# Two attention blocks on one core: eleven loads of V described as 8 blocks of 4 rows instead of 32 rows

## The chip, the core and the metric

The kernel runs on one core of one Trainium2 chip. Beside the four compute engines (PE, the matrix engine; DVE, the vector engine; ACT, the scalar engine; POOL) the core has a sequencer SP, which here issues nearly all transfers, and sixteen DMA engines that carry them between the chip's memory (HBM) and the on-chip buffers (SBUF). The metric is the device time in microseconds; the time before is the median of three runs, 840.8 us (840.2 to 841.24).

## The reference

Two attention blocks, A and B, on separate inputs; their outputs stand side by side in the result. Both project a batch of 16 x 32 tokens to 32 query heads, attend to a cache of 1024 keys with heads of 128, and project back to 1024 columns. They differ in the cache: A has 4 key/value heads, each used by 8 query heads; B has 32 of its own.

```python
q = (x @ wq).reshape(B, Sq, H, Dh).transpose(0, 2, 1, 3)
scores = jnp.einsum("bhqd,bhkd->bhqk", q, k_cache) * (Dh ** -0.5)
p = softmax(scores)
o = jnp.einsum("bhqk,bhkd->bhqd", p, v_cache)
out = o.transpose(0, 2, 1, 3).reshape(B, Sq, H * Dh) @ wo
...
return jnp.concatenate([a, b], axis=-1)
```

All data are bf16. B's two caches are 134 MB each (16 x 32 x 1024 x 128 x 2 bytes), A's 17 MB each, so the kernel reads 338 MB in one pass.

## The kernel before

The work is cut into 128 steps for each attention. A step of B, a *quad*, handles four (batch, head) pairs with 32 queries each, which together fill the 128 partitions: scores into two PSUM banks (L1040), the row maximum on DVE (L1051), the exponential on ACT (L1064), a transposition of the probabilities on PE (L1076), their copy to SBUF (L655), the product with V (`st_pvB`, L1109), the normalisation and a transposition of the result. After each group of quads the output projection follows (L827). A's steps are alike and are set between B's.

The order of the instructions on each engine is not the order of the source. `list_schedule` simulates the engines with a table of durations and picks, engine by engine, what goes next; SP's queue is ordered by it too. It knows a transfer by its name and its bytes (`dma_time`, by `vb_dma` for the loads here), not by how its source is described. Semaphores are then placed by `finalize`.

**The loads.** SP issues about a thousand transfers, all on one queue (`qSPDynamicHW`), each as soon as its buffer is free; it waits in order, so a load whose buffer is not free holds up all those behind it. `load` (L625) is the helper for the caches and the output weights. It regards `fold` neighbouring rows of the source as one longer row. For a tile of V, 128 rows of 2048 bytes (the 8 keys of a partition, 128 values each), with `fold` 4, the source is described as 32 rows of 8192 bytes, and the destination as 128 partitions of 2048 bytes. The source is one piece of 256 KB without gaps in any case.

**V of B.** There are 512 such loads, numbered `y` from 0 to 511; quad `t` uses y = 4t to 4t + 3, one for each of its four pairs. `st_dmaVB` (L965) emits them. `home_v` gives the buffer: up to y = 419 one of twelve slots of `VB_sb`, later also the room that the token buffers leave free (`xT_sb`, `QT_sb`), and for the last eight loads that of K tiles (`KB_sb`). The four loads of a quad share a semaphore (`sem_v`), and PE waits for all four before L1109. A slot is loaded again when PE has finished the product that read it.

Of the kernel before, what the change touches and what calls it, by code (L numbers as in the profile page):

```python
# [7 lines left out]
ALU = alu_op_type.AluOpType  # L8
# [549 lines left out]
def build(nc, pa, pb, out):  # L558
# [9 lines left out]
    NCH = Sk // P  # L568
# [4 lines left out]
    MS = 4  # L573
# [17 lines left out]
    pr = Prog()  # L591
    stack = contextlib.ExitStack()
    with stack:
# [28 lines left out]

        psum = ps("psum", [P, 8, 512], F32)

        def load(e, dst, src, fold):  # L625

            if fold == 1:
                return e.dma_start(dst, src)
            return e.add_instruction(mybir.InstDMACopy(  # L629
                name=nc.get_next_instruction_name(), engine=mybir.EngineType.SP, queue="qSPDynamicHW", mode="Copy",  # L630
                ins=e.lower_ap_dma(src.rearrange("(p r) x -> p (r x)", r=fold)), outs=e.lower_ap_dma(dst), cce_op=ALU.bypass))

        def bank(v):
            return psum[:, v.idx, :]
# [158 lines left out]
        def wo_loadA(s_):  # L793
            wo = pa["wo"]
            for h_ in range(HS):
                r0 = (s_ * HS + h_) * Dh

                def th(h_=h_, r0=r0):
                    pr.add("sp", lambda e: load(e, woA_sb[:, h_, :], wo[r0:r0 + Dh, :], 4),
                           writes=[("woA", h_)], dma_key=f"woA{h_}", name="woA_dma", dur=Dh * D * 2, wtag={("woA", h_): s_})  # L800
                lazy_push(("wo", 0, s_), th)

        def wo_loadB(m_):
            wo = pb["wo"]
            for h_ in range(MS):
                r0 = (m_ * MS + h_) * Dh

                def th(h_=h_, r0=r0):
                    pr.add("sp", lambda e: load(e, woB_sb[:, h_, :], wo[r0:r0 + Dh, :], 4),
                           writes=[("woB", h_)], dma_key=f"woB{h_}", name="woB_dma", dur=Dh * D * 2, wtag={("woB", h_): m_})  # L810
                lazy_push(("wo", 1, m_), th)
# [79 lines left out]
        def st_dmaKA(q):  # L891
            if not q.kv_new:
                return
            sl = q.kvslot
            pr.add("sp", lambda e: load(e, KA_sb[:, sl, :, :].rearrange("p c d -> p (c d)"), pa["k"][q.b, q.s].rearrange("(p c) d -> p (c d)", c=NCH), 4),
                   writes=[("KA", sl)], dma_key=f"ka{sl}", name="ka_dma", dur=Sk * Dh * 2, wtag={("KA", sl): q.kid})
# [26 lines left out]
        def home_v(y):  # L923
            x, h = y // 2, y % 2
            if x >= V_LAST:
                return (("KB", "KBh")[h], kb_of(x - 8))
            if x < XV:
                return ("VB", 2 * (x % NVB) + h)
            r = (x - XV) % (NVB + 4)
            return ("xV" if r < 2 else "QV", 2 * (r % 2) + h) if r < 4 else ("VB", 2 * ((XV + r - 4) % NVB) + h)  # L930
# [19 lines left out]
        def tile_v(y):  # L950
            kind, sl = home_v(y)
            if kind == "xV":
                return xT_sb[:, 1, :, :].rearrange("p (i j) t -> p i (j t)", i=4)[:, sl, :]
            if kind == "QV":
                return QT_sb[:, 0, :, :, :].rearrange("p (i b) a q -> p i (b a q)", i=4)[:, sl, :]
            if kind in ("KB", "KBh"):
                h = int(kind == "KBh")
                return KB_sb[:, sl, h * NCH * Dh:(h + 1) * NCH * Dh]
            return VB_sb[:, sl, :]

        def sem_v(y):
            kind, sl = home_v(y - y % 4)
            return {"VB": sl // 4, "xV": NVB, "QV": NVB + 1}.get(kind, NVB + 2 + sl)

        def st_dmaVB(y):  # L965
            kind, sl = home_v(y)
            q, x = quadsB[y // 4], y % 4
            pr.step, was = 2 * ((y // 2 - NVB) // 4) if y // 2 >= NVB else pr.step, pr.step
            pr.add("sp", lambda e: load(e, tile_v(y), pb["v"][q.b0 + x // 2, q.m * MS + 2 * (x % 2) + q.e].rearrange("(p s) d -> p (s d)", s=NCH), 4),
                   writes=[(kind, sl)],  # L970
                   dma_key="v%d" % sem_v(y), name="vb_dma", dur=Sk * Dh * 2, wtag={(kind, sl): ("V", y)})
            pr.step = was
# [182 lines left out]
        def pairB(n):  # L1155
            qs = [quadsB[2 * n], quadsB[2 * n + 1]]
            for x in range(4):
                st_ktrB(4 * n + x)
            if n == 0:
                for x in range(4, NKB):  # L1160
                    st_dmaKB(x)
            st_scoresB(qs)
            while k_next[0] < min(2 * NIT, 4 * n + 4 + NKB + (4 if n >= LATE else 0)):
                st_dmaKB(k_next[0])
                k_next[0] += 1
            if 4 * n == V_LAST - 8:
                for y in range(8):
                    st_dmaVB(2 * V_LAST + y)
            for q in qs:
                st_max(q)  # L1170
                st_exp(q)
                st_ptr(q)
                st_pev(q)
                st_pvB(q)
                while v_next[0] < min(2 * V_LAST, 4 * q.t + 4 + 2 * NVB + (8 if n >= LATE else 0)):
                    st_dmaVB(v_next[0])
                    v_next[0] += 1
                st_recip(q)
                st_norm(q)
                st_otr(q)  # L1180
# [34 lines left out]
        for y in range(8):  # L1215
            st_dmaVB(y)
# [86 lines left out]
        if SCHED:  # L1303
            pr = pr.list_schedule()
# [41 lines left out]
```

## Time and profile before

| | |
|---|---|
| median of three runs | 840.8 us (840.2 to 841.24) |
| the profiled execution, its own time | 841.83 us |
| its span, first to last instruction | 840.0 us |
| granted clock of PE, mean | 0.99 |
| read from HBM | 337.64 MB |
| loads of V of B into `VB_sb` | 468 of 256 KB, median 7.5 us from issue to landing |

The profile is one execution on the chip. Its page gives the busy time of each engine, the span in forty slices, the DMA queues with the share of sixteen engines' time that their packets took, the chain of waits that ended last, and the costliest groups of instructions; finer views answer for a stretch of time, a tile or a line of the source. Queue q1 is SP's; q0 carries the seven stores that POOL issues; q8 and q14 bring the engines' own instructions. A packet of 4 bytes is the completion that one DMA engine writes to a load's semaphore when its share is done, and in this trace there are sixteen for each of the 1009 transfers that SP and POOL issue (16144 packets under 512 bytes). "DMA share" in a window is the mean busy share of the sixteen DMA engines; a packet is counted where it starts, so in short windows the share can pass 1.

### The profile page before, as it was taken

How to read it: one execution, taken by the hardware profiler on the slowest of the kernel's cores; microseconds unless marked ns; L12 is line 12 of the kernel's file. 1: busy time of each engine (PE TensorE's matmuls, PEld its weight loads, DVE VectorE, ACT ScalarE, POOL GpSimd, SP SyncE). 2: the span in 40 equal slices, each digit the busy share in tenths (PEclk: the TensorE clock that was granted, in tenths of full speed). 3: DMA queues.
4: the chain of work that ended last, by engine and by line, in shares of the span. 5: the costliest groups of instructions: out<-in, count | busy, mean ns of one | idle time of the engine just before them, and what ended most of it. 6: DMA issues, size and time to landing. Idle time of an engine off the chain costs nothing.

```text
span 840.0 us, 29458 instructions
## 1 busy us (share of the span) xinstructions
PE 732.0 (87%) x12732; PEld 470.6 (56%) x12864; DVE 721.5 (86%) x1021; ACT 608.4 (72%) x1356; POOL 5.0 (1%) x15
## 2 busy tenths in 40 slices
PE   6979989898889889988998988988889988789776
PEld 3446655655656555655556555565646656466553
DVE  1688888979979888988998898998899889988994
ACT  4368878867768785877678786685867877687764
POOL 0000000000000000000000000000000000000000
PEclk9999999999999999999999999999999999999999
DMA  9999999999999999999999999999999999999995
GB/s 336 420 419 414 416 418 418 414 414 410 404 418 415 416 417 419 396 415 416 418 410 410 411 415 419 417 415 402 405 419 400 415 417 419 416 418 417 418 390 224
DMA packets 65104, 341.68 MB, mean 407 GB/s; under 512 B 16144, under 2 KB 16400, under 8 KB 26064
## 3 DMA queue, kind: packets, MB, share of 16 engines
q1 hardware_dynamic: 64416, 337.97, 98.6%
q8 instruction: 101, 1.65, 0.8%
q0 software_dynamic: 560, 1.84, 0.5%
q14 instruction: 27, 0.22, 0.1%
HBM read 337.64 MB, written 2.10 MB: 404 GB/s over the span
## 4 chain that ended last, share of the span: by engine, by line
PE 37%; DMA 22%; DVE 21%; ACT 12%; SPq 4%; issue 3%; ACTq 0%
DMA KB_sb<-in_B_k_cache_dram 14%; DVE stat L1051 9%; DVE KB_sb L991 9%; ACT P_sb L1064 8%; PE psum L1076 7%; PE psum L827 6%; DMA VB_sb<-in_B_v_cache_dram 5%; PE psum L1040 5%; PE psum L758 4%; PE psum L1109 3%; PE psum L1096 3%; SPq L629 3%; PE psum L739 2%; PE psum L1010 2%; ACT PT_sb L655 2%
## 5 line engine op out<-in xcount | busy, mean ns | idle before, releaser
L1051 DVE TENSOR_REDUCE stat<-psum 128x1 f32<-128x1024 f32 x256 | 301.8, 1206 | 38.5 <-PE psum L1040 22.7
L1064 ACT ACTIVATE P_sb<-psum,stat 128x1024 bf16<-128x1024 f32 x246 | 275.0, 1120 | 56.8 <-DVE stat L1051 55.3
L991 DVE STREAM_TRANSPOSE KB_sb<-KB_sb 128x1024 f32<-128x1024 f32 x240 | 287.2, 1224 | 21.5 <-DMA KB_sb<-in_B_k_cache_dram 21.1
L1076 PE MATMUL psum<-id,P_sb 128*128 128x128 f32 x984 | 167.9, 300 | 22.4 <-ACT P_sb L1064 20.2
L1076 PEld LDWEIGHTS psum<-id,P_sb 128*128 128x128 f32 x984 | 138.6, 209 | 59.6 <-ACT P_sb L1064 43.3
L655 ACT COPY PT_sb<-psum 128x512 f32<-128x512 f32 x230 | 131.4, 597 | 34.5 <-PE psum L1076 33.0
L1125 ACT ACTIVATE O_sb<-psum,stat 128x128 bf16<-128x128 f32 x198 | 72.2, 373 | 41.2 <-PE psum L1096 21.5
L1096 PE MATMUL psum<-VA_sb,PT_sb 128*128 128x128 bf16 x1024 | 78.3, 220 | 8.9 <-ACT P_sb L1064 1.7
L1040 PE MATMUL psum<-KB_sb,QR 32*32 32x512 bf16 x3840 | 75.2, 394 | 5.4 <-ACT P_sb L1064 2.8
L1096 PEld LDWEIGHTS psum<-VA_sb,PT_sb 128*128 128x128 bf16 x1024 | 62.0, 98 | 31.1 <-ACT PT_sb L655 9.2
L1010 PE MATMUL psum<-KTA_sb,QT_sb 128*128 128x512 bf16 x201 | 68.2, 388 | 10.8 <-ACT P_sb L1064 5.1
L1109 PE MATMUL psum<-VB_sb,PT_sb 128*32 128x128 bf16 x3584 | 67.9, 223 | 7.6 <-DMA VB_sb<-in_B_v_cache_dram 3.2
L758 PE MATMUL psum<-wq_sb,xT_sb 128*128 128x512 bf16 x231 | 65.2, 389 | 8.0 <-issue 2.7
L827 PE MATMUL psum<-woB_sb,OTB_sb 128*128 128x512 bf16 x240 | 64.8, 386 | 6.4 <-DMA woB_sb<-in_B_wo_dram 1.4
L1109 PEld LDWEIGHTS psum<-VB_sb,PT_sb 128*32 128x32 bf16 x3584 | 52.7, 98 | 26.8 <-issue 8.4
L827 PE MATMUL psum<-woA_sb,OTA_sb 128*128 128x512 bf16 x245 | 59.7, 380 | 4.6 <-issue 1.3
L1040 PEld LDWEIGHTS psum<-KB_sb,QR 32*32 32x32 bf16 x3840 | 42.6, 89 | 31.4 <-ACT P_sb L1064 7.4
L1132 PE MATMUL psum<-ident,O_sb 128*128 128x128 bf16 x256 | 49.0, 225 | 10.4 <-ACT O_sb L1125 5.9
L739 PE MATMUL psum<-xT_sb,wq_sb 128*128 128x512 bf16 x170 | 48.5, 379 | 2.8 <-issue 1.4
L1064 ACT ACTIVATION_READ_ACCUMULATOR P_sb<-psum,stat 128x1 f32 x246 | 49.9, 203 | 0.0
L839 DVE TENSOR_TENSOR acc<-acc,psum 128x512 f32<-128x512 f32 x64 | 40.9, 673 | 9.0 <-PE psum L827 8.7
L1132 PEld LDWEIGHTS psum<-ident,O_sb 128*128 128x128 bf16 x256 | 23.4, 98 | 39.9 <-ACT O_sb L1125 17.2
(64 smaller groups left out, 586.7 us busy)
## 6 DMA issues: line engine op xcount, KB each, us to landing
KB_sb<-in_B_k_cache_dram SPq DMA_DIRECT2D x240, 512.0 KB, 9.7
VB_sb<-in_B_v_cache_dram SPq DMA_DIRECT2D x468, 256.0 KB, 7.5
KA_sb<-in_A_k_cache_dram SPq DMA_DIRECT2D x64, 256.0 KB, 8.4
VA_sb<-in_A_v_cache_dram SPq DMA_DIRECT2D x64, 256.0 KB, 8.6
wq_sb<-in_B_wq_dram SPq DMA_DIRECT2D x16, 512.0 KB, 9.5
woB_sb<-in_B_wo_dram SPq DMA_DIRECT2D x32, 256.0 KB, 8.5
woA_sb<-in_A_wo_dram SPq DMA_DIRECT2D x32, 256.0 KB, 7.1
wq_sb<-in_B_k_cache_dram SPq DMA_DIRECT2D x16, 512.0 KB, 10.7
```

Of the source, the lines that this page charges most:

```text
L655: return e.copy(dst, src) if hasattr(e, "activation") else e.tensor_copy(dst, src)
L758: last = e.matmul(bank(v)[:, 0:CW], xT_sb[:, 1, j, G * P:(G + 1) * P], wq_sb[:, j, mh * CW:(mh + 1) * CW], start=(j == 0), stop=(j == DJ - 1))
L827: last = e.matmul(bank(v)[:, 0:OUTW], OT[:, gp, hh, :], wo_[:, hh, oh * OUTW:(oh + 1) * OUTW], start=(hh == 0), stop=(hh == nh - 1))
L991: pr.add("dve", lambda e: e.transpose(tile_k(x).bitcast(F32), tile_k(x).bitcast(F32)), writes=res_k(x), name="KBt_tr", rtag={home_k(x): x} ...
L1010: pr.add("pe", lambda e, u=u: e.matmul(bank(vS[u]), qt[:, q.b, q.hh0:q.hh0 + 4, :].rearrange("p a q -> p (a q)"), KTA_sb[:, sl, u * 512:(u ...
L1040: last = e.matmul(bank(q.vS[g2])[32 * x:32 * x + 32, :].rearrange("p (s j) -> p s j", s=16), lhsT, rhs, start=(fp == 0), stop=(fp == 3), t ...
L1051: pr.add("dve", lambda e: e.tensor_reduce(stat[:, vst.idx, 0:1], both(vS), AXIS.XY, ALU.max, negate=True), writes=vS + [vst], name="max")
L1064: return e.activation(dst, src, ACTF.Exp, bias=stat[:, vst.idx, 0:1], scale=1.0, accum_out=stat[:, vst.idx, 1:2])
L1076: last = e.transpose(bank(vb)[:, m * P:(m + 1) * P], p32[:, m:Sk // 2:NPK], id32[:])
L1096: last = e.matmul(bank(vb)[:, 0:Dh], ptc_of(vPT, c, 0, P), VA_sb[:, kvs, c, :], start=(c == 0), stop=(c == NCH - 1))
L1109: last = e.matmul(bank(vb)[32 * x:32 * x + 32, 0:Dh], ptc_of(vPT, c, 32 * x, 32 * x + 32), tile_v(4 * q.t + x)[:, c * Dh:(c + 1) * Dh], st ...
L1132: pr.add("pe", lambda e: e.transpose(bank(vb)[:, 256:320].bitcast(BF), O_sb[:, vO.idx, :], ident[:]), reads=[vO, "ident"], writes=[vb], na ...
```

## The change

`load` gets a parameter `half`. Where it is set, the same source is described with one more dimension: 8 blocks of 4 rows of 8192 bytes, instead of 32 rows of 8192 bytes; the destination gets a dimension of size 1 between partitions and columns, so that both have three. `st_dmaVB` sets it for y = 20, 68, 116, ..., 500, every 48th, eleven loads in all. Nine of them go to slot 8 of `VB_sb` (y = 20 to 404), one to slot 4 (y = 452) and one to `xT_sb` (y = 500); each is the first of the four loads of its quad.

```diff
-        def load(e, dst, src, fold):
+        def load(e, dst, src, fold, half=False):
 
             if fold == 1:
                 return e.dma_start(dst, src)
+            if half:
+                rows, tile = src.rearrange("(h p r) x -> h p (r x)", h=8, r=fold), dst.rearrange("p (o x) -> p o x", o=1)
+            else:
+                rows, tile = src.rearrange("(p r) x -> p (r x)", r=fold), dst
             return e.add_instruction(mybir.InstDMACopy(
                 name=nc.get_next_instruction_name(), engine=mybir.EngineType.SP, queue="qSPDynamicHW", mode="Copy",
-                ins=e.lower_ap_dma(src.rearrange("(p r) x -> p (r x)", r=fold)), outs=e.lower_ap_dma(dst), cce_op=ALU.bypass))
+                ins=e.lower_ap_dma(rows), outs=e.lower_ap_dma(tile), cce_op=ALU.bypass))
...
-            pr.add("sp", lambda e: load(e, tile_v(y), pb["v"][q.b0 + x // 2, q.m * MS + 2 * (x % 2) + q.e].rearrange("(p s) d -> p (s d)", s=NCH), 4),
+            pr.add("sp", lambda e: load(e, tile_v(y), pb["v"][q.b0 + x // 2, q.m * MS + 2 * (x % 2) + q.e].rearrange("(p s) d -> p (s d)", s=NCH), 4, y % 48 == 20),
                    writes=[(kind, sl)],
```

The same bytes go to the same places, on the same queue, in the same order, and with the same semaphores.

## The prediction

> **What bounds the kernel now.** I read the page from the top, then the DMA view over the steady stretch from 100 to 700 us, then SP's waits, then short windows in which the DMA engines are not all busy.
>
> ```profile
> span 840.0 us, 29458 instructions
> PE 732.0 (87%) x12732; PEld 470.6 (56%) x12864; DVE 721.5 (86%) x1021; ACT 608.4 (72%) x1356; POOL 5.0 (1%) x15
> ...
> DMA  9999999999999999999999999999999999999995
> ...
> DMA packets 65104, 341.68 MB, mean 407 GB/s; under 512 B 16144, under 2 KB 16400, under 8 KB 26064
> ## 3 DMA queue, kind: packets, MB, share of 16 engines
> q1 hardware_dynamic: 64416, 337.97, 98.6%
> q8 instruction: 101, 1.65, 0.8%
> q0 software_dynamic: 560, 1.84, 0.5%
> q14 instruction: 27, 0.22, 0.1%
> ...
> PE 37%; DMA 22%; DVE 21%; ACT 12%; SPq 4%; issue 3%; ACTq 0%
> ```
>
> No compute engine is full (87%, 86%, 72%), but the DMA engines are: the shares of the four queues add to 100.0% of sixteen engines' span, from the second slice to the last but one. The chain of waits is mixed, 37% PE and 22% DMA, because each side releases the other: a transfer waits for a buffer that PE frees, PE waits for the transfer. What decides the length of such a loop is the part that never rests, and that is the transfers.
>
> ```profile
> DMA packets 46497, 247.75 MB, mean 413 GB/s; under 512 B 11695, under 2 KB 11695, under 8 KB 17903
> ## 3 DMA queue, kind: packets, MB, share of 16 engines
> q1 hardware_dynamic: 46321, 246.09, 100.4%
> q8 instruction: 75, 1.23, 0.8%
> ...
> VB_sb<-in_B_v_cache_dram SPq DMA_DIRECT2D x368, 256.0 KB, 7.3
> ```
>
> This is the DMA view from 100 to 700 us. It moves 413 GB/s, 25.8 GB/s an engine. (Shares pass 100% because neighbouring packets overlap a little.) The loads of q1 are dealt evenly, as far as bytes go; queue q8, PE's own code, need not be. Its 75 fetches of 16 KB take 0.8% of 16 x 600 us, 77 us, which is 1.02 us each.
>
> ```profile
> core 0: us, PE busy (x) PEld busy (x) DVE busy (x) ACT busy (x) POOL busy (x), PEclk, DMA share, GB/s
> 800.00:801.00 1.00, 1.00 (x29) 0.65 (x27) 1.00 (x2) 0.85 (x3) 0.00 (x0) 1.00 0.94 385
> 801.00:802.00 1.00, 0.95 (x10) 0.57 (x8) 1.00 (x1) 0.37 (x1) 0.00 (x0) 1.00 0.64 254
> ...
> 826.00:827.00 1.00, 1.00 (x9) 0.95 (x8) 0.90 (x3) 1.00 (x3) 0.00 (x0) 1.00 1.02 410
> 827.00:828.00 1.00, 0.62 (x6) 0.48 (x4) 1.00 (x5) 1.00 (x4) 0.09 (x1) 1.00 0.96 381
> 828.00:829.00 1.00, 0.86 (x39) 0.56 (x41) 0.40 (x1) 0.98 (x3) 0.45 (x1) 1.00 0.59 238
> ```
>
> These windows are the row that matters most. The DMA share (the column before GB/s) does not sink slowly at the end of the loads: it is 1.02 and 0.96, then 0.59 in one step. 0.59 of sixteen is 9.4 engines; about half are through while the other half still has work. The same step, 0.64, stands at 801 to 802 us, where SP is late with the next load. So the engines form two halves, and one runs behind. I also followed the single packets of the trace, which no view prints, from one packet's end to the next one's start: all 101 fetches of q8 fall on the same eight engines, one after the other in a fixed round, and the 27 of q14 on the others. That makes **the eight engines that also fetch PE's code the bound of the kernel**: 101 x 1.02 us / 8 = 12.9 us of work each that the other eight do not have. I call them the late half.
>
> [...]
>
> **The change part by part.** Bytes, buffers, semaphores, order and number of issues stay. What moves is how one load is dealt out.
>
> *The dealing.* Now a V load is 32 source rows of 8192 B, two for each of sixteen engines, 16384 B each; at 25.8 GB/s that is 0.635 us. The trace of before has no load described by eight blocks. Bound from both sides: either the dealing follows the rows, and nothing changes, 0 us; or it follows the outermost count, and then eight engines carry four rows each and eight carry none. I take the second, since nothing but the outermost count is different. Each such load then gives 0.635 us more to eight engines and takes 0.635 us from the other eight; eleven make 7.0 us each way.
>
> [...]
>
> *Which half.* This is the step on which the sign hangs, and no row of the profile names the engines by number. If the late half loses the eleven shares, its work shrinks by 7.0 us and the other half's grows by 7.0, out of the 12.9 us that it has to spare: the halves then differ by 12.9 - 14.0, about nothing, and the bound sinks by 6.5 to 7.0. If the late half gets them, its work grows by 7.0. I take the first, by judgement and not by a reading, and keep the second as the main rival.
>
> *What of the 7.0 us arrives.* A shorter transfer stage helps only where loads are issued in time.
>
> ```profile
> SPq L629 <- PE psum L1109: 65.0, 39, 4.9
> SPq L629 <- PE psum L984: 29.4, 20, 5.7
> SPq L629 <- PE psum L1132: 23.1, 29, 3.2
> SPq L629 <- PE psum L827: 20.7, 25, 3.5
> ```
>
> ```profile
> 791.87 3.20 SPq L629 DMA_DIRECT2D VB_sb<-in_B_v_cache_dram  x4
> 800.89 2.83 SPq L629 DMA_DIRECT2D wq_sb<-in_B_k_cache_dram  x4
> ```
>
> SP waits for PE to free buffers, 65.0 us at the PV matmuls alone. Mostly this is covered, as the queue holds some 7 us of loads (the 7.3 us from issue to landing above). Where SP waits longer the quick half runs dry: after its issue at 791.87 + 3.20 = 795.07 it waits 5.8 us, until 800.89, and one us at 801 misses 0.36 of sixteen engines, 0.7 us on each engine of the dry half. There the late half has still been busy; once it is no longer late, it runs dry too. The bound: no such spell costs anything (gain 7.0), or some seven spells of that size do (gain 7.0 - 5.0 = 2.0). I take three of them, 2.0 us: nearer the first end, since the tenths of DMA show a 9 in all slices but the last, so long spells are rare. Gain 5.0.
>
> *Issue.* SP spends about 0.6 us on a load.
>
> ```profile
> L629 SPq DMA_DIRECT2D VB_sb<-in_B_v_cache_dram x468: 471/594/1816, 16.1 to 812.4; - x156
> ...
>   DMA VB_sb<-in_B_v_cache_dram: 10.6, 16
> ...
> DMA to landing us min/median/max: 4.3/7.5/13.2
> ```
>
> The V loads took 0.471 to 1.816 us to issue, median 0.594. If the three-dimensional description costs the extremes, eleven make between -1.4 and +13.4 us of SP's time, spread over 800 us. It hides behind the 7.5 us of median lead from issue to landing, and SP's own waits; without that cover it would be paid in full. I take the median, 0.
>
> *Landing.* A load on eight engines takes 1.27 us instead of 0.635. Behind it on its engines stand the K loads and the next V tiles; PE waits for it, then ACT and DVE for PE. On the half that is ahead by 0.64 us or more it lands no later; if it always landed late and PE always waited, 11 x 0.635 = 7.0 us. PE has waited for these tiles 16 times, 10.6 us in all, so most are not waited for. I take 0.
>
> *The sum.* The profiled execution took 841.83 us, 1.03 above the median of the three shown runs (840.8); its span is 840.0, with 1.8 around it. 841.83 - 7.0 + 2.0 = 836.8 for it, and 840.8 - 5.0 = **835.8 us** on the scale of the median. The case's own range is 833.8 (all 7.0 arrive) to 838.8 (2.0 arrive).
>
> **The rivals.**
>
> *The late half gets the blocks.* Same dealing, other side. For it: nothing in the profile forbids it, and half the ways of numbering give it. The late half never rests (its engines are the ones still at work in the 0.59 window), so every added 0.635 us is paid from the first such load on: 840.8 + 7.0 = **847.8 us**. It decides as soon as the eight engines of the blocks include any that fetch PE's code, so a numbering in which the halves are mixed ends here too. Against it: only my judgement. [...]
>
> *The description dissolves.* The eight blocks lie one behind the other in memory, so they may be joined again to 32 rows before the packets are made; then 840.8. Against it: the 32 rows lie as densely and are not joined today, since packets under 8 KB are only 17903 of 46497 and the V loads keep rows of 8192 B.
>
> *Compute takes over.* The late half is relieved, but buffers come free no sooner: the chain's 37% PE and 21% DVE close the gap, and SP's waits (65.0 us and the others) grow by what the transfers win. Then 840.8 - 1.0 = 839.8. Against it: the engines' 87% and 86% leave room, and the transfers have none.
>
> **How the numbers follow.** Forecast 0.62, late half gets the blocks 0.27, dissolved 0.06, compute takes over 0.05. Faster by over 0.2% (1.7 us, about what a measurement of this kernel can tell from no change): 0.62. Within it: 0.06 + 0.05 = 0.11. Slower: 0.27. The range from 833.0 to 848.0 takes in the forecast's own 833.8 to 838.8, the two middle cases, and the rival's 847.8 but not the part of it in which late landings or issues add to the 7.0; that part, with what lies below 833.0, is under 0.2. Since it spans both signs: if the forecast's case holds, 833.8 to 838.8.
>
> **What would show it.** The dealing: packets under 512 B (one completion for each engine and load) fall from 16144 by 11 x 8 = 88, while bytes and the large packets stay; if they stay 16144, the description dissolved. The half: in the last us of the loads the DMA share no longer stands near 0.6 but falls from about 1 to 0 within one us if the late half was relieved; if it was loaded, the share near 0.5 lasts some microseconds longer than now, and such steps appear at more places. What arrives: SP's waits for PE grow by no more than a few us and its issues of V stay near 0.594. I would be wrong in the mechanism if the time moved while the completions did not fall, and in the sign alone if they fall by 88 and the time is near 848.

## The result and the profile after

The changed kernel takes 865.0 us (median of 4 runs, 863.45 to 866.24), the kernel before 840.5 (839.61 to 841.24): a ratio of 1.0285, 95% interval 1.0267 to 1.0302. It is slower by 24.5 us, 2.2 us for each of the eleven loads. The forecast was 835.8, and the range ended at 848.

The page of the changed kernel, the lines that answer to those of before:

```profile
span 864.3 us, 29590 instructions
PE 757.8 (88%) x12864; PEld 476.0 (55%) x12864; DVE 723.4 (84%) x1021; ACT 609.1 (70%) x1356; POOL 5.1 (1%) x15
...
DMA  9999999999999999999999999999999999999994
...
DMA packets 65016, 341.68 MB, mean 395 GB/s; under 512 B 16056, under 2 KB 16312, under 8 KB 25976
## 3 DMA queue, kind: packets, MB, share of 16 engines
q1 hardware_dynamic: 64328, 337.97, 98.1%
q8 instruction: 101, 1.65, 0.7%
...
PE 41%; DMA 27%; DVE 16%; ACT 11%; SPq 4%; issue 2%; ACTq 0%
```

The packets under 512 B fell from 16144 to 16056, by 88 = 11 x 8. So the change did what it says: each of these loads runs on eight DMA engines. The bytes are the same. But the packets of q1, added up one by one and divided by sixteen, took 847.5 us (98.1% of 864.3), where they took 828.6 us (98.6% of 840.0). That is **18.8 us more transfer time on the average engine for the same bytes**, and no moving of work from one engine to another can do that: it changes the parts, not the mean.

The DMA view from 100 to 700 us says it in another way; before, it had 46321 packets and 246.09 MB at 100.4%:

```profile
DMA packets 45295, 241.18 MB, mean 402 GB/s; under 512 B 11293, under 2 KB 11293, under 8 KB 17501
## 3 DMA queue, kind: packets, MB, share of 16 engines
q1 hardware_dynamic: 45123, 239.56, 100.2%
```

The share is as full as before, and 6.5 MB less went through. Two-microsecond windows after one of the changed loads (issued at 530.1 us) show where; the last two columns are the DMA share and GB/s:

```profile
core 0: us, PE busy (x) PEld busy (x) DVE busy (x) ACT busy (x) POOL busy (x), PEclk, DMA share, GB/s
532.00:534.00 2.00, 2.00 (x41) 0.91 (x40) 1.88 (x6) 1.29 (x5) 0.00 (x0) 1.00 1.04 430
534.00:536.00 2.00, 2.00 (x55) 0.95 (x54) 1.51 (x4) 1.22 (x3) 0.00 (x0) 1.00 1.03 397
536.00:538.00 2.00, 1.84 (x62) 1.28 (x34) 1.53 (x3) 0.76 (x4) 0.00 (x0) 1.00 0.99 266
538.00:540.00 2.00, 1.84 (x9) 0.80 (x10) 2.00 (x2) 2.00 (x4) 0.00 (x0) 1.00 1.02 299
540.00:542.00 2.00, 2.00 (x15) 1.42 (x14) 2.00 (x4) 1.37 (x4) 0.00 (x0) 1.00 1.01 377
```

For some 6 us all sixteen engines are busy and move 266 to 377 GB/s instead of 413: the engines are not idle, their packets take longer. Such a dip follows each of the eleven loads: of the windows of 2 us in the 14 us behind its issue the lowest has 254 to 356 GB/s; in the kernel before, behind the same loads, none is under 372. In the single packets, which no view prints, those of 8192 B that took over 330 ns (most take 309 to 315) rose from 441 to 2631, counted from 30 us on: 199 for each changed load, which has 32 packets itself. So the loads around it are slowed too.

The end of the loads, in windows of 1 us:

```profile
848.00:849.00 1.00, 1.00 (x10) 1.00 (x8) 0.90 (x2) 1.00 (x3) 0.00 (x0) 1.00 0.85 348
849.00:850.00 1.00, 0.62 (x5) 0.43 (x5) 0.99 (x5) 1.00 (x4) 0.01 (x1) 1.00 0.50 201
850.00:851.00 1.00, 0.91 (x35) 0.61 (x34) 0.48 (x1) 1.00 (x3) 0.53 (x1) 1.00 0.19 78
851.00:852.00 1.00, 0.79 (x33) 0.55 (x33) 0.00 (x0) 0.57 (x2) 0.00 (x0) 1.00 0.75 295
852.00:853.00 1.00, 0.78 (x33) 0.58 (x33) 0.00 (x0) 0.48 (x3) 0.00 (x0) 1.00 0.12 49
853.00:854.00 1.00, 0.04 (x4) 0.00 (x0) 0.00 (x0) 0.37 (x1) 0.00 (x0) 1.00 0.12 49
854.00:855.00 1.00, 0.00 (x0) 0.00 (x0) 0.00 (x0) 0.00 (x0) 0.00 (x0) 1.00 0.08 33
```

A part of these shares is not loads but the stores that POOL issues (q0). The DMA view of a single window tells the two apart. This is the window of the 0.59 before, 828 to 829 us:

```profile
q1 hardware_dynamic: 29, 0.16, 37.9%
q0 software_dynamic: 31, 0.08, 20.6%
```

And this is the changed kernel from 849 to 850 us:

```profile
q0 software_dynamic: 44, 0.14, 35.5%
q1 hardware_dynamic: 15, 0.06, 14.2%
```

So before, the loads themselves held 0.38 of sixteen engines (and 0.34 in the next microsecond): the time of six, on six engines or on more that carry packets of the store in between. Now they hold 0.14 from 849 to 851 us and 0.12 from there to 853. From 852 to 853 nothing else runs, and 0.12 of sixteen is the time of **two engines**; so read, these two work alone until 855 us. The group that trailed before is gone, but not as I had forecast: fourteen engines are level, and two are some 5 us behind them. The run with six changed loads, below, ends in the same way (a share of 0.12 from 841 to 842 us).

PE waits longer for the tiles of V, 21.6 us where it was 10.6 (the view of the tile `VB_sb`):

```profile
  DMA VB_sb<-in_B_v_cache_dram: 21.6, 18
```

SP, in the view of waits, waits for PE at the product with V as long as before (65.0 us then):

```profile
SPq L633 <- PE psum L1113: 66.8, 37, 4.4
```

### The profile page after: what moved, and what is told of

Read it like the earlier page. It is cut to its first block, busy times and chain, and to the rows that moved or that the text cites. A ratio compares the mean times of both kernels' runs of the same rounds, so it can differ in the third digit from the quotient of the medians.

```text
span 864.3 us, 29590 instructions
## 1 busy us (share of the span) xinstructions
PE 757.8 (88%) x12864; PEld 476.0 (55%) x12864; DVE 723.4 (84%) x1021; ACT 609.1 (70%) x1356; POOL 5.1 (1%) x15
## 2 busy tenths in 40 slices
DMA packets 65016, 341.68 MB, mean 395 GB/s; under 512 B 16056, under 2 KB 16312, under 8 KB 25976
## 3 DMA queue, kind: packets, MB, share of 16 engines
q1 hardware_dynamic: 64328, 337.97, 98.1%
q8 instruction: 101, 1.65, 0.7%
## 4 chain that ended last, share of the span: by engine, by line
PE 41%; DMA 27%; DVE 16%; ACT 11%; SPq 4%; issue 2%; ACTq 0%
DMA KB_sb<-in_B_k_cache_dram 10%; DMA VB_sb<-in_B_v_cache_dram 8%; PE psum L1080 7%; DVE stat L1055 7%; ACT P_sb L1068 7%; PE psum L831 6%; DVE KB_sb L995 6%; PE psum L1044 5%; PE psum L762 4%; PE psum L1113 4%; PE psum L1100 3%; PE psum L743 3%; PE psum L1014 3%; DMA VA_sb<-in_A_v_cache_dram 3%; SPq L633 3%; DMA KA_sb<-in_A_k_cache_dram 3%
## 5 line engine op out<-in xcount | busy, mean ns | idle before, releaser
L1080 PE MATMUL psum<-id,P_sb 128*128 128x128 f32 x984 | 170.1, 303 | 24.6 <-ACT P_sb L1068 22.7
L1014 PE MATMUL psum<-KTA_sb,QT_sb 128*128 128x512 bf16 x256 | 83.0, 389 | 10.5 <-ACT P_sb L1068 6.9
L762 PE MATMUL psum<-wq_sb,xT_sb 128*128 128x512 bf16 x256 | 72.3, 396 | 5.7 <-DMA wq_sb<-in_B_wq_dram 2.8
L831 PE MATMUL psum<-woB_sb,OTB_sb 128*128 128x512 bf16 x256 | 68.7, 387 | 4.0 <-DMA woB_sb<-in_B_wo_dram 1.4
L831 PE MATMUL psum<-woA_sb,OTA_sb 128*128 128x512 bf16 x256 | 61.9, 380 | 4.4 <-ACT P_sb L1068 2.8
L743 PE MATMUL psum<-xT_sb,wq_sb 128*128 128x512 bf16 x192 | 53.2, 380 | 0.6 <-ACT OTB_sb L659 0.4
```

The costliest lines, as they stand in the source:

```text
L743: last = e.matmul(bank(v)[:, 0:tn], w_[:, j, hh * Dh:(hh + 1) * Dh], xT_sb[:, 0, j, t0:t0 + tn], start=(j == 0), stop=(j == DJ - 1))
L762: last = e.matmul(bank(v)[:, 0:CW], xT_sb[:, 1, j, G * P:(G + 1) * P], wq_sb[:, j, mh * CW:(mh + 1) * CW], start=(j == 0), stop=(j == DJ - 1))
L831: last = e.matmul(bank(v)[:, 0:OUTW], OT[:, gp, hh, :], wo_[:, hh, oh * OUTW:(oh + 1) * OUTW], start=(hh == 0), stop=(hh == nh - 1))
L1014: pr.add("pe", lambda e, u=u: e.matmul(bank(vS[u]), qt[:, q.b, q.hh0:q.hh0 + 4, :].rearrange("p a q -> p (a q)"), KTA_sb[:, sl, u * 512:(u ...
L1080: last = e.transpose(bank(vb)[:, m * P:(m + 1) * P], p32[:, m:Sk // 2:NPK], id32[:])
```

## The experiments

Two causes are supposed. P: an engine that writes to other partitions than it usually does is in the way of the engine that usually writes there, and both are slower; no view shows which engine writes where. D: the dealing to eight engines, that is imbalance. Beside them the form of the description (F) and the reading side (H). Losses are against the kernel before on the same chip, in the same series; slow packets are those of 8192 B over 330 ns, 441 in the trace of before (- where the rows of the loads in question have another size).

| run | time, us | loss, us | ratio, 95% interval | slow packets |
|---|---|---|---|---|
| changed kernel | 865.0 | 24.5 | 1.0267 to 1.0302 | 2631 |
| 16 blocks of 2 rows | 857.9 | 16.2 | 1.0158 to 1.0204 | 2433 |
| 32 blocks of 1 row | 841.6 | -0.2 | 0.999 to 1.0017 | 472 |
| 16 rows of 16384 B, two dimensions | 856.0 | 14.2 | 1.0153 to 1.0199 | - |
| 8 blocks, rows apart in the source | 863.3 | 21.6 | 1.0229 to 1.027 | 2356 |
| 4 blocks of 8 rows | 870.4 | 28.7 | 1.0323 to 1.0358 | 2782 |
| 8 blocks, six loads | 854.0 | 12.3 | 1.0124 to 1.0157 | 1581 |
| halves of 64 partitions | 848.7 | 6.9 | 1.0066 to 1.0105 | 1700 |
| quarters of 32 partitions | 862.6 | 20.8 | 1.0217 to 1.0317 | 1833 |
| all loads in 16 rows | 1210.6 | 369.2 | 1.4295 to 1.4489 | - |
| all V of B in 16 rows | 1236.7 | 395.3 | 1.4636 to 1.475 | - |
| added loads, partitions 0 to 63 | 850.1 | 8.7 | 1.0084 to 1.0119 | 658 |
| added loads, partitions 16 to 47 and 80 to 111 | 856.3 | 15.2 | 1.015 to 1.0191 | 2065 |

### Form, dealing or place

Sixteen blocks, the same form, all sixteen engines:

```diff
-                rows, tile = src.rearrange("(h p r) x -> h p (r x)", h=8, r=fold), ...
+                rows, tile = src.rearrange("(h p r) x -> h p (r x)", h=16, r=fold), ...
```

> The same eleven loads, in the same three-dimensional form, but as 16 blocks of 2 rows of 8192 B, so that sixteen engines carry two rows each again. If the form costs (theory F), the time stays at 865.0 us. If it is the dealing to eight engines that costs (theory D: 24.5 us / 11 = 2.2 us per changed load), it returns to 840.5 us, within 1 us, with 16144 packets under 512 B. If what costs is that an engine writes to other partitions than it usually does (theory P), it lies between, by how far 16 blocks differ from 32 rows there.

It took 857.9. From 100 to 700 us there are 11482 packets under 512 B; 16 for each of the 718 transfers issued there make 11488, and with 8 for the eight loads of 16 blocks among them it would be 11424. So, by this count, sixteen engines carry each load, as before, and two thirds of the loss stay. The greater part of it is not imbalance, then.

Thirty-two blocks of one row (`h=32` at the same place):

> The three-dimensional form with 32 blocks of one row of 8192 B, that is the rows of the kernel before with the extra dimensions of the changed one. If the form costs (F), it stays near the 857.9 of 16 blocks or the 865.0 of 8. If what costs is which engine writes which partitions (P), 32 rows are dealt as before and the time is that of the kernel before, 841.7 within 1.5 us.

841.6, 0.2 us under the kernel before: the third dimension alone costs nothing here, F is out.

The other way round, no third dimension, but two neighbouring rows for an engine:

```diff
-... load(e, tile_v(y), pb["v"][...].rearrange("(p s) d -> p (s d)", s=NCH), 4),
+... load(e, tile_v(y), pb["v"][...].rearrange("(p s) d -> p (s d)", s=NCH), 8 if y % 48 == 20 else 4),
```

> The two-dimensional form of the kernel before, but the eleven loads as 16 rows of 16384 B, so that one engine has the two rows of 8192 B that lie together, as with 16 blocks. No extra dimension. If the form costs (F), nothing changes against before: 841.7. If who writes which partitions costs (P), it is as with 16 blocks: 857.9, within 1.5 us, with the same 16144 packets under 512 B and about as many slow packets of 8192 B.

856.0, and the interval overlaps that of the 16 blocks. What the two descriptions share is only that two neighbouring rows stand together in a block or a row; by the reading of P an engine has both of them. With 32 rows, by the difference in time, it does not have them so.

The reading side, by a block that takes every eighth row of the source and writes to the same partitions as in the changed kernel:

```diff
-                rows, tile = src.rearrange("(h p r) x -> h p (r x)", h=8, r=fold), ...
+                rows, tile = src.rearrange("(p h r) x -> h p (r x)", h=8, r=fold), ...
```

> Again 8 blocks of 4 rows, but a block takes every eighth row of the source (rows 64 KB apart) instead of four that lie together; the destination is described as in the changed kernel. The keys of these eleven tiles of V then stand in another order, so the output is not the reference's. If the piece of 32 KB that one engine reads in a row is what costs (theory H, the reading side), the time changes by several us, towards 845 to 855. If the cost lies in the dealing to eight or in the writing side (D, P), it stays at 865, within 1.5 us.

863.3: of the 24.5 us at most some 3 hang on how the source is read (its interval just touches that of the changed kernel). So most of the cost is not on the reading side; by P it is on the writing side.

### How the loss grows

> 4 blocks of 8 rows: four engines with 8 rows each, 12 more packets under 512 B missing per load (16144 - 132 = 16012). By the sum of my prediction, without any contention, a changed load costs its four engines 2 rows x 3 more = 1.9 us more than their share, 21 us in all: 861 if they are of the late half, 848 if not. If contention grows with the rows that one engine carries (D), it is well above that: twice the loss of the changed kernel or more, 890. If it grows with the number of engines that write elsewhere (P), the loss stays near 24 us, 865.

With `h=4` it is 870.4, which none of the numbers named meets. The slow packets (2782) are hardly more than with 8 blocks, as P has it, and 12.5 to 14.5 us more than with 16 blocks come on top, under the 21 us of four engines that are all late; which of the four are late I did not resolve.

> The changed form on every 96th load, six instead of eleven. If each changed load costs the same (2.2 us), 840.5 + 6 x 2.2 = 853.9 us. If the first few are covered by the 12.9 us that one half has to spare and only the later ones cost, it is under 850. If one such load would upset the order of the engines for good, it stays near 865.

With `y % 96 == 20` it is 854.0: 12.3 / 6 = 2.0 us a load against 24.5 / 11 = 2.2, and 190 more slow packets a load against 199. From six loads to eleven the loss is additive; no sign shows of loads that the slack of one half covers.

### The same rows in other pieces

The eleven loads as two (or four) transfers of 64 (or 32) partitions, in the form of before, each with its own 16 counts on the semaphore:

```diff
...
+                n = 2 if y % 48 == 20 else 1
+                return [load(e, dst[i * P // n:(i + 1) * P // n], src[i * P // n:(i + 1) * P // n], 4) for i in range(n)]
...
```

> The eleven loads as two transfers of 64 partitions each, in the form of before, 16 rows of 8192 B: each engine has one row of each, so every engine carries as much as before, and eleven more issues of some 0.6 us. If only the load on the engines counts (D), 841.7 to 843. If the partitions count (P), some engines write where others usually do: half of the rows if the engine follows the partition number with a step of 4, then about half of the loss of 16 blocks, 841.7 + 8 = 850; completions rise by 176 to 16320.

848.7 and 1700 slow packets. From 100 to 700 us there are 11709 packets under 512 B; 16 for each of the 734 transfers issued there make 11744, and with 8 for the 16 halves among them it would be 11616. So, by this count, sixteen engines carry each half of 16 rows, and still there is a loss, a little under half that of the 16 blocks. This was the expectation of P for a dealing in which an engine takes groups of four partitions; that dealing is assumed, no run shows it.

> The eleven loads as four transfers of 32 partitions, 8 rows each. Eight rows can only go to eight engines, so eight engines carry four rows each, as in the changed kernel, but in another order: an engine has every eighth row instead of four that lie together. Completions: 16144 + 11 x 16 = 16320. If the number of engines decides (D), 865. If the partitions decide (P) and at least the lower half goes to the engines that usually write it, clearly less: 850 to 857.

862.6 with a wide interval, above the 850 to 857 of P. From 100 to 700 us there are 11552 packets under 512 B for 735 transfers, 32 of them quarters: 16 for each would make 11760, 8 for each quarter 11504. So eight engines carry a quarter, and if all four quarters go to the same eight, the imbalance is that of the changed kernel. The slow packets are fewer (1833 against 2631), but 33 more issues are in it as well, and what each of these contributes stays open.

### Is the tie fixed?

All loads of the caches and output weights in 16 rows (`fold` 8 everywhere), so that none is dealt differently from its neighbours:

> The form of the kernel before, two dimensions, but every load of the caches and of the output weights has 16 source rows (16384 B for V, A's K and V and the weights, 32768 B for B's K), so that all of them are dealt to the engines in one and the same way, that of the sixth run. If the cost comes from loads that are dealt differently from their neighbours (an engine writes where another one writes at that time), it is gone: 841.8 within 3 us. If certain engines are tied to certain partitions and every other dealing costs (fixed), it is much slower, by 100 us and more.

The page of this kernel:

```profile
span 1205.3 us, 29458 instructions
...
DMA packets 41552, 341.68 MB, mean 283 GB/s; under 512 B 16144, under 2 KB 16400, under 8 KB 26064
...
q1 hardware_dynamic: 40864, 337.97, 98.6%
```

1210.6 us, at a share as full as ever, on all sixteen engines (16144 completions) and with larger packets: 283 GB/s instead of 407. So the trouble is not that one load is unlike the others. This is what was expected if **certain engines are tied to certain partitions** and the dealing that 32 rows bring is the one that fits; the last run below shows with the sizes kept that the place counts (6.2 us).

> Only the loads of V of B have 16 rows of 16384 B, all 512 of them; K and the rest as before. By either theory half of the traffic now is dealt differently from the other half. If each such load costs the 14.2 / 11 = 1.3 us of the sixth run, 841.8 + 512 x 1.3 = 1507 us. If packets can't wait longer than the time for which two engines share, the loss saturates: up to 1100 us. If the dealing alone is harmless when it is steady, below 900.

1236.7 us from two runs, which is neither the 1507 us of a loss that adds up nor under the 1100 us of one that saturates early. With less than half of the bytes in 16 rows the loss is far below 512 x 1.3 us, and the mean rate of 277 GB/s is about that with all of them (283). Here the packets of q1 fill only 91.2% of the span, so some of the engines' time is idle; why, stays open.

How the rows of a usual load are dealt to the engines, which engine writes which partitions, and why a packet written elsewhere should take longer, no run shows. What the runs give is the size of the loss by the pieces of the eleven loads: 6.9 us for halves of 64 partitions, 14.2 and 16.2 us for two rows that lie together, -0.2 us for single rows.

### Which engines, and which places

The kernel before with 32 more loads, of 48 KB each, to a spare tile:

```diff
...
+                if y % 32 == 20:
+                    d += [load(e, spare[i * 32:(i + 1) * 32], flat[i * 192:(i + 1) * 192].rearrange("(p s) d -> p (s d)", s=6), 4) for i in range(2)]
...
```

> The kernel before, and behind every 32nd load of V (16 of them) two more loads of 48 KB, each to 32 partitions (0 to 31, 32 to 63) of a spare tile that nothing reads: 8 rows of 6144 B, so eight engines, 0.24 us each (6144 B at 25.8 GB/s): 16 x 2 x 0.24 = 7.6 us more work for those eight engines, and 32 more issues. It asks on which side the eight engines of a load of 8 rows lie. If they are not the late half, the 7.6 us fit in the 12.9 us that they have to spare: 842 to 844. If they are the late half, all is paid: 841.8 + 7.6 = 849.4. Completions: 16144 + 32 x 8 = 16400.

850.1: the whole 7.6 us is paid and 1.1 us more, and yet the eight engines are not the late half. The added packets are the only ones of 6144 B in the trace, so their eight engines can be told. In 11 of the 16 places six of the eight start on them within 1.5 us of each other, and **two start 2.9 to 4.2 us after the first**. Followed from one packet's end to the next one's start, three chains reach a fetch of q8, and each comes from one of the two latest of its eight (at 528.9 us from both); six chains of 30 to 53 us of the others reach none. (I take q8 for PE's code by its size: in the kernel before it brings 1.65 of the 1.87 MB of instructions, 88%, and PE and PEld have 25596 of the 29458 instructions, 87%. Eight engines share 101 fetches in 840 us, so each has one about every 67 us: a chain of that length can miss one, but hardly all six.) The fetches of q14, which lie on the other engines, are reached by four chains, three of them from quick ones. So, as far as these chains show, of the eight engines that an 8-row load uses two fetch PE's code and six don't: the halves are mixed. That the two late ones pay for the added rows is the reading that fits; the slow packets rose here too (441 to 658), and the run does not separate what of the 8.7 us is the rows' own time and what is slower packets.

The same with the places shifted by 16 partitions:

```diff
-                    d += [load(e, spare[i * 32:(i + 1) * 32], ...
+                    d += [load(e, spare[16 + i * 64:48 + i * 64], ...
```

> The run before with the added loads, changed in one thing: the 32 added loads of 48 KB go to partitions 16 to 47 and 80 to 111 of the spare tile instead of 0 to 31 and 32 to 63. The same bytes, sizes, engines and issues. If each engine is tied to certain partitions (P), all added rows are now written by engines that do not usually write there: 256 rows at about 0.04 us each (the halves' run: 6.9 us for 176 rows), 850 + 10 = 860, and more than 1500 packets of 8192 B over 330 ns instead of 658. If the place does not matter, 850.1 again, within 1.5 us.

856.3, 6.2 us more than at partitions 0 to 63 (10 were expected, at 0.04 us for a row of 8192 B, an estimate that takes half of the halves' 352 rows for rows written elsewhere, which no run shows; these have 6144 B, which makes 7.5), and the slow packets rise from 658 to 2065. The source, the bytes, the sizes and the issues are the same; only the partitions differ. Eight engines carry each added load in either run: the first has 16401 packets under 512 B, where 16144 + 32 x 8 make 16400, and here there are 11653 from 100 to 700 us, where 8 for each of the 24 added loads and 16 for the other 713 transfers make 11600, and 16 for all 11792. That the place alone costs time shows here most plainly; P is the reading that fits it.

None of the thirteen kernels is faster than the one before.

## Why the prediction was wrong

**The bound** held. The transfers set the time, before and after. Its size was read a little high: packet by packet the 101 fetches took 101.0 us, 12.6 us on each of eight engines instead of 12.9. And the row that mattered most did not show by itself what I read from it: of its 0.59, 0.21 was POOL's store, and 0.38 of loads is less than half of the engines. (In the window at 801 us no store runs, and that reading stands.) A group that trails is there again where all sixteen engines carry the same (16 blocks, in its windows at the end):

```profile
842.00:843.00 1.00, 0.56 (x44) 0.38 (x35) 0.00 (x0) 0.75 (x2) 0.00 (x0) 1.00 1.01 410
843.00:844.00 1.00, 0.62 (x30) 0.39 (x18) 0.00 (x0) 0.47 (x2) 0.00 (x0) 1.00 0.58 238
844.00:845.00 1.00, 0.73 (x33) 0.49 (x32) 0.00 (x0) 0.44 (x2) 0.00 (x0) 1.00 0.49 201
845.00:846.00 1.00, 0.00 (x0) 0.00 (x0) 0.00 (x0) 0.14 (x1) 0.00 (x0) 0.92 0.44 168
846.00:847.00 1.00, 0.00 (x0) 0.00 (x0) 0.00 (x0) 0.00 (x0) 0.00 (x0) 0.50 0.10 41
```

The loads themselves have 0.48 and 0.44 from 843 to 845 us, with 0.10 and 0.05 of the store beside them, so that about half of the engines trail, as I had read it. That the engines which trail are those with the code fetches rests on the chains of packets above.

**The dealing** was half right. Eight engines with four rows each, 88 completions fewer: right. The step that failed is the price, "0.635 us more to eight engines and takes 0.635 us from the other eight". It took a packet's time as the same wherever it is written, so that the sum over all engines could not change, and it grew by 18.8 us on the average engine. Bounding the dealing by "0 us" and "four rows each" left out what the experiments point to: a dealing is also a choice of who writes where. With all engines loaded alike (16 blocks) that alone cost 14.2 to 16.2 us. The sum had no term for it, and neither had any rival, so the true time lay outside the range.

**Which half** failed as well, as a question: there is no such half. The rival "the late half gets the blocks" had in one clause what was so, that a numbering in which the halves are mixed ends on its side. By that reading six late engines were relieved, which fits that the group is gone; two got the blocks on top of their fetches, the two that work alone until 855 us. Its price of 7.0 us is somewhat above what is left for it: the span of the profiled execution grew by 24.3 us, the packets' time on the average engine by 18.8, so that at most the 5.5 us between are engines that end unlevel. With 16 blocks the packets' time grew by 15.1 us (828.6 to 843.7), so the step from 16 blocks to 8 made the packets slower by another 3.7. Why four rows that lie together cost more than two was not tested.

**What of the 7.0 us arrives**: nothing did, so the 2.0 us that I took off for spells of late issue were not tested. **Issue at the median** was nearly right: the changed loads took 0.644 to 0.724 us to issue, the same eleven loads before 0.471 to 0.612, which is 1.5 us over all eleven, beside SP's waits of 66.8 us at one line alone. **Landing at 0** was wrong in size. PE's wait for V rose by 11.0 us (10.6 to 21.6), though the runs do not separate what of it is the landing of a changed load and what the slower packets of the loads around it.

**The check signs** served: the 88 completions settled the dealing at once. The share at the end read neither way that I had named, and it had been set by the window with POOL's store in it; the new reading (0.12, two engines) gave the mixed halves. A sign for the case that happened, the bytes moved in a window with a full share, was missing.

## What to carry to other kernels

How a load was described moved the time of this kernel, by the reading of P because it decides which DMA engine writes which partitions: two rows that lie together cost 1.3 to 1.5 us for each load of 256 KB in a stream that keeps the engines full, with the same bytes and issues; four rows on half of the engines cost 2.2 us, the imbalance included. In the profile the sign was a full DMA share with fewer GB/s (100.2% at 402 GB/s from 100 to 700 us, against 100.4% at 413), so read the two columns together; a share near 1 does not say that the engines are doing their best. Before work is moved between engines to level them, look whether it can be moved at all. Counting all 11 x 32 = 352 rows of the changed loads as written elsewhere, a row cost 6.9 / 352 = 0.02 us in halves of 64 partitions and 16.2 / 352 = 0.046 us in 16 blocks, and more if fewer rows were; to take half of the 12.9 us off eight engines, 6.5 x 8 / 0.31 = 168 rows would have to move, and by this estimate they cost 3.3 us at the rate of the halves and 7.7 us at that of the 16 blocks, against the 6.5 us that they bring.

## What the hardware showed

- A load of 48 KB to 32 partitions on eight engines took SP longer to issue (median 0.687 us) than a whole one of 256 KB (0.594 us):

```profile
L631 SPq DMA_DIRECT2D spare<-in_B_v_cache_dram x32: 677/687/764, 55.6 to 823.2; - x32
```

- Larger packets did not help: with all loads in rows of 16384 B and 32768 B a packet of 16384 B took 893 ns on average, where two of 8192 B take 632 in the kernel before.
- The 101 fetches of q8, 1.65 MB, by their size PE's code, fall on eight engines, followed from packet to packet. As far as the chains show, two of them are among the eight that an 8-row load uses, and so six among the others.
